# Doubles turned into floats with two VectorE operations a tile instead of four, and block sums and splits of the second MLP's input in smaller, spread pieces

## The chip, the core and the metric

The program runs on one core of a Trainium2 chip. Its time is that of one execution on the device in microseconds (us); lower is better. An execution was also recorded by the hardware profiler, and all rows below come from that one record.

The engines are TensorE (PE in the profile, with PEld for its weight loads), VectorE (DVE), ScalarE (ACT), GpSimd (POOL) and SyncE (SP), which here only issues DMAs. Each engine runs its own instructions in order; semaphores tie the engines together.

## The reference

```python
def _attn_ref(q, k, v, p):                       # (8, 8, 576, 64), p: (8, 8, 32, 64)
    def sm_attn(qq, kk, vv):
        s = scale * np.matmul(qq, kk.transpose(0, 1, 3, 2))
        s = s - np.max(s, axis=-1, keepdims=True)
        a = np.exp(s)
        a = a / (np.sum(a, axis=-1, keepdims=True) + 1e-09)
        return np.matmul(a, vv)
    p_packed = sm_attn(p, k, v)
    return sm_attn(q, p_packed, p_packed)

def _moe_ref(x, w_gate, w_val, w_out, rms_g):    # x: (4608, 512), d_ff 1536
    rms = np.sqrt(np.mean(x * x, axis=-1, keepdims=True) + 1e-06)
    xn = x / rms * rms_g
    g = xn @ w_gate
    silu = g * (1.0 / (1.0 + np.exp(-g)))
    return (silu * (xn @ w_val)) @ w_out

def _moe2_ref(x, w_in, w_out):                   # d_ff 2048
    h = x @ w_in
    g = h * (1.0 / (1.0 + np.exp(-1.702 * h)))
    return g @ w_out
```

Attention goes into MLP one, that into MLP two. The five weight matrices arrive as 64-bit floats, everything else as 32-bit floats; the output has 32-bit floats.

## The kernel before

The first part runs attention for four pairs of batches, and beside it MLP one: `prods` (L661) forms the products of the packed values with the gate and value weights (`ps_w`), `gateval` (L699) multiplies them by the attention weights (`ps_g`), and `project` (L737) applies `w_out` (`ps_o`) and adds into `acc`. Nearly every matmul operand is split into a high part (ScalarE's cast to `fp32r`) and a low part (a subtraction on VectorE or GpSimd), and three matmuls replace one.

The weights become floats in `words` (L119). A double is read as two 32-bit words, `top` and `low`. ScalarE writes |top| to the SBUF tile `w` (L127). VectorE takes the maximum with a least value into `m` (L128), shifts left by 5 and right by 2 (L129), puts the two uppermost bits of `top` back (L130), and joins three bits of `low` (L131), which writes `w`. `m`, named `between`, is a PSUM bank out of the pool `mm` of five banks, the same five that `ps_w`, `ps_g` and `ps_o` take. For the last pair of blocks of MLP two, which is converted while MLP two already runs, there is no such bank and `m` is `w` itself. `convert` (L134) calls `words` for 36 pieces of MLP one's weights, then ScalarE (L140) and GpSimd (L141) split `w`; `weights` (L851) calls it for 32 pieces of MLP two's. `raw` has three buffers, `w` two.

MLP two (`main`, L987) uses seven block products instead of eight for each of its two matrix products. It works on five spans of tokens, three of 2 x 512 and two of 2 x 384, and each span goes in four turns. A turn has 14 up steps (`up`, L1035: six matmuls into a bank `ps_up`) and seven down steps (`down`, L1101: 24 or 18 matmuls into banks `ps_dn`), interleaved by `form_at` and `down_at`; the down steps of a turn come during the turn after it. VectorE empties the banks (L1064 to L1073, L1149), and `form` (L1078) prepares the left operands (L1087 to L1091, L1095, L1096).

The input of a span is `b11`, `b12`, `b21`, `b22`, loaded by `load_x` (L1006), and the sums `t1 = b12 - b11`, `t3 = b22 - b12`, `t2 = b22 - t1`, `t4 = b21 - t2`. `prepare(s + 1, q)` (L1017) makes block `q` of the next span directly after the last up step that reads `q` of this one: in the last seven up steps of a span. It also computes the sums there, in place (L1024, L1028, L1029, L1031), and splits each whole block of 128 x 1024 or 128 x 768 with one ScalarE copy (L935) and one subtraction (L936), on GpSimd for `b11`, `b21`, `b22` and on VectorE for `t1` to `t4`.

In the last turn of a span, after down step 1, three additions on GpSimd add `acc["u"]` to three quarters of the result (L1150 to L1153). Steps 5 and 6 send the result out.

The order within each engine is made by a planner that simulates the program when it is built; it may move an instruction ahead of others that were written earlier, where its inputs and its buffers are there.

Of the kernel before, what the change touches and what calls it, by code (L numbers as in the profile page):

```python
# [9 lines left out]
F32 = mybir.dt.float32  # L10
F32R = mybir.dt.float32r
I32 = mybir.dt.int32
AF = mybir.ActivationFunctionType
ALU = mybir.AluOpType
# [2 lines left out]
DRAM = bass.MemoryType.DRAM  # L17


LEAST_WORD = 2.0**-15  # L20
GELU = 1.702


def fl(t):

    return t.bitcast(F32)
# [3 lines left out]
def tile_pack_attention__then__two_mlps(  # L30
# [14 lines left out]
    nc = tc.nc  # L45
# [9 lines left out]
    P = 128  # L55
# [29 lines left out]
    NGR = NP2 // 2  # L85
    TH = 512
    WHOLE = 3
    HALF = DM // 2
    spans = [(i * 2 * TH, TH) for i in range(WHOLE)]
# [29 lines left out]
    def words(pool, r, n, banks=None, bufs=2):  # L119

        top, low = r[:, :, 1], r[:, :, 0]
        w = pool.tile([P, n], I32, tag="w", name="w", bufs=bufs)
        wf = w.bitcast(F32)
        m = w if banks is None else banks.tile([P, 512], I32, tag="mm", name="between")[:, :n]
        nc.scalar.activation(wf, top.bitcast(F32), AF.Abs)  # L127
        nc.vector.tensor_scalar(m.bitcast(F32), wf, LEAST_WORD, None, op0=ALU.max)  # L128
        nc.vector.tensor_scalar(m, m, 5, 2, op0=ALU.logical_shift_left, op1=ALU.logical_shift_right)  # L129
        nc.vector.scalar_tensor_tensor(m, top, -(1 << 30), m, op0=ALU.bitwise_and, op1=ALU.bitwise_or)  # L130
        nc.vector.scalar_tensor_tensor(w, low, 29, m, op0=ALU.logical_shift_right, op1=ALU.bitwise_or)  # L131
        return w

# [697 lines left out]
    def mlp2(cv):  # L831
# [85 lines left out]
        def x_tile(q, n=TH):  # L917
            xb[q] = pools["pre"].tile([P, 2, 2, TH], F32R, tag=q, name=f"x_{q}", bufs=1)[:, :, :, :n]
            return xb[q]
# [13 lines left out]
        def split_x(q, src, engine, n=TH):  # L933
            t = x_tile(q, n)
            nc.scalar.copy(t[:, 0], src)  # L935
            engine.tensor_sub(t[:, 1], src, fl(t[:, 0]))  # L936
# [50 lines left out]
        def main(wp, sp, pm, pa, later):  # L987
            turns = [(s, g) for s in range(len(spans)) for g in range(NGR)]
            ups = [(t, a, q) for t in range(len(turns)) for a in range(2) for q in product_order]
            PER = 2 * len(product_order)  # L990
# [7 lines left out]
            def load_wo(d):  # L998
                if d < 7 * len(turns):
                    t, j = divmod(d, 7)  # L1000
                    wo[d] = wp.tile([P, 2, 2, HALF], F32R, tag="wo", name="wo2", bufs=WOB)
                    nc.sync.dma_start(fl(wo[d]), wo2_d[turns[t][1]][:, down_blocks.index(down_order[j][1])])

            xr = {}

            def load_x(s):  # L1006
                if s < len(spans):
                    t0, n = spans[s]
                    for q, i0, k in (("b11", 0, 0), ("b12", 0, 1), ("b22", 2, 1), ("b21", 2, 0)):
                        if q == "b21":  # L1010
                            t = wp.tile([P, 2, TH], F32, tag="xr", name="xr", bufs=1)
                        else:
                            t = cv.tile([P, 2, TH], F32, tag="raw", name="xr", bufs=RAWS)
                        xr[q] = t[:, :, :n]
                        load_part(xr[q], i0, t0 + k * n, n)

            def prepare(s, q):  # L1017

                if s == len(spans):
                    return  # L1020
                n = spans[s][1]
                b11, b12, b21, b22 = (xr[x] for x in ("b11", "b12", "b21", "b22"))
                if q == "t2":
                    nc.vector.tensor_sub(b11, b22, b11)  # L1024
                source = {"t1": "b11", "t2": "b11", "t3": "b12", "t4": "b21"}.get(q, q)
                split_x(q, xr[source], nc.gpsimd if q in ("b11", "b21", "b22") else nc.vector, n)
                if q == "b11":
                    nc.vector.tensor_sub(b11, b12, b11)  # L1028
                    nc.vector.tensor_sub(b12, b22, b12)  # L1029
                elif q == "b21":  # L1030
                    nc.vector.tensor_sub(b21, b21, b11)  # L1031

            g, bank, u2 = {}, {}, {}

# [64 lines left out]
            acc, banks = {}, {}  # L1099

            def down(d):  # L1101

                t, j = divmod(d, 7)
                s, gr = turns[t]
                t0, n = spans[s]
                per = n // P
                first, last = gr == 0, gr == NGR - 1
                which = "AB" if t % 2 == 0 else "BA"
                name, go_on = which[(0, 1, 0, 1, 0, 1, 0)[j]], j in (2, 5, 6)
                parts = [(r, min(2, per - r)) for r in range(0, per, 2)]  # L1110
                if not go_on:
                    banks[name] = [
                        pa.tile([P, 2, HALF], F32, tag=f"dn{name}{i}", name="ps_dn", bufs=1) for i in range(len(parts))
                    ]
                oh, ol = formed.pop(d)
                w = wo.pop(d)
                for o, (r0, m) in zip(banks[name], parts):
                    i = 0
                    for r in range(m):
                        for a in range(2):  # L1120
                            for x, y in ((oh, 0), (oh, 1), (ol, 0)):
                                nc.tensor.matmul(  # L1122
                                    o[:, r],
                                    x[:, a, (r0 + r) * P : (r0 + r + 1) * P],
                                    w[:, a, y],
                                    start=i == 0 and not go_on,
                                    stop=i == 6 * m - 1,
                                    skip_group_check=True,
                                )
                                i += 1  # L1130
                if first and j == 0:
                    for k in range(2):
                        acc[k] = sp.tile([P, TH // P, DM], F32, tag=f"acc{k}", name="acc2", bufs=1)
                    acc["u"] = sp.tile([P, TH // P, HALF], F32, tag="accu", name="accu", bufs=1)
                target, begins = {
                    0: ("u", True), 1: ("u", False), 2: ((0, 0), True), 3: ((1, 1), True),
                    4: ((1, 1), False), 5: ((0, 1), True), 6: ((1, 0), True),
                }[j]
                if target == "u":
                    to = acc["u"]  # L1140
                else:
                    k, c = target
                    to = acc[k][:, :, c * HALF : (c + 1) * HALF]
                for o, (r0, m) in zip(banks[name], parts):
                    z = to[:, r0 : r0 + m]
                    if first and begins:
                        nc.scalar.copy(z, o[:, :m])
                    else:
                        nc.vector.tensor_add(z, z, o[:, :m])  # L1149
                if last and j == 1:  # L1150
                    for k, c in ((1, 1), (0, 1), (1, 0)):
                        z = acc[k][:, :per, c * HALF : (c + 1) * HALF]
                        nc.gpsimd.tensor_add(z, z, acc["u"][:, :per])  # L1153
                if last and j >= 5:
                    k = j - 5
                    for r0, m in parts:
                        at0 = t0 + k * n + r0 * P
                        nc.sync.dma_start(
                            out[at0 : at0 + m * P, :].rearrange("(r p) d -> p r d", p=P), acc[k][:, r0 : r0 + m]
                        )  # L1160
# [2 lines left out]
                load_wi(c)  # L1163
            for d in range(WOB):
                load_wo(d)
            form_at, down_at = {}, {}
            for d in range(7 * len(turns)):
                t, j = divmod(d, 7)
# [3 lines left out]
            for c in range(len(ups) + PER + LAG):  # L1172
                if c < len(ups):
                    up(c)
                    load_wi(c + WIB)
                    if c >= 7:
                        next(later, None)
                    if c % PER == 6 and turns[ups[c][0]][1] == NGR - 2:
                        load_x(turns[ups[c][0]][0] + 1)
                for d in form_at.get(c, ()):  # L1180
                    form(d)
                for d in down_at.get(c, ()):
                    down(d)
                    load_wo(d + WOB)
# [4 lines left out]
    with ExitStack():  # L1189
# [8 lines left out]
        cv = ctx.enter_context(tc.tile_pool(name="cv", bufs=1, side="left"))  # L1198
        with ExitStack() as st1:
# [56 lines left out]
            u, ahead, calm, since = 0, None, 0.0, 0.0  # L1256
# [95 lines left out]
```

## Time and profile before

| | |
|---|---|
| time, median of 3 runs | 1658.5 us (1656.1 to 1660.7) |
| the profiled execution | 1658.6 us |
| its span, first to last instruction | 1656.7 us |
| busy share of the span | PE 97%, PEld 92%, DVE 70%, ACT 52%, POOL 56% |
| mean granted TensorE clock | 0.992 of full speed |
| moved by DMA | 348.21 MB, 210 GB/s on the mean |

Busy shares are means over stages of different kind. A wait names the instruction that was late and the one that released it. The granted clock is given as a share of full speed; 0.5 stands for the lower of the two levels, 1.2 GHz, and 1.0 for the upper, 2.4 GHz.

### The profile page before, as it was taken

The numbers are of one execution on the slowest core, as the hardware profiler recorded it, in microseconds if no ns is written. First come the engines' busy times: TensorE is split into PE (matmuls) and PEld (weight loads), VectorE is DVE, ScalarE is ACT, GpSimd is POOL, SyncE is SP. The second block draws the span as 40 slices with busy tenths as digits, with TensorE's granted clock in tenths as the row PEclk, the third lists the DMA queues.
The fourth block names the chain that finished last, engine by engine and source line by source line (L and its number), as shares of the span: only waits on it lengthen the run. The fifth ranks groups of instructions, "written<-read, shape, count | busy, mean of one in ns | idle before, by whom it ended". The sixth has DMA issues, their size and how long they took to land.

```text
span 1656.7 us, 29176 instructions
## 1 busy us (share of the span) xinstructions
PE 1611.8 (97%) x10608; PEld 1516.4 (92%) x10608; DVE 1161.9 (70%) x2004; ACT 866.7 (52%) x1771; POOL 928.8 (56%) x744
## 2 busy tenths in 40 slices
PE   7899999999999999999999999999999999999997
PEld 5689998999999999999999889899989999999997
DVE  5788988877768777686886476864585458567564
ACT  4667776666566666665655344434344434434432
POOL 2447777656666557562665266564456446546444
PEclk8999999999999999999999999999999999999999
DMA  9655666584565855465445878676667667887874
GB/s 256 178 163 173 205 189 221 190 254 150 167 204 204 271 186 186 148 207 205 167 177 175 293 259 268 218 245 187 188 207 242 192 186 243 281 250 237 286 222 127
DMA packets 217726, 348.21 MB, mean 210 GB/s; under 512 B 93936, under 2 KB 123632, under 8 KB 211440
## 3 DMA queue, kind: packets, MB, share of 16 engines
q1 hardware_dynamic: 217584, 346.35, 65.1%
q8 instruction: 85, 1.39, 0.3%
q14 instruction: 57, 0.47, 0.1%
HBM read 279.19 MB, written 67.11 MB: 209 GB/s over the span
## 4 chain that ended last, share of the span: by engine, by line
PE 77%; DVE 11%; issue 3%; POOL 3%; DMA 3%; ACT 3%; SPq 0%; POOLq 0%; DVEq 0%; ACTq 0%
PE ps_dn L1122 18%; PE ps_up L1051 18%; PE ps_o L748 15%; PE ps_g L712 13%; PE ps_w L679 3%; PE ps_at L308 3%; PE ps_at L353 2%; PE ps_at L297 2%; PE ps_at L443 2%; DMA vn<-in_v_dram 1%; DVE x_t L936 1%; DVE Wl L684 1%; DVE w L131 1%; POOL Hl L734 0%; DVE between L128 0%
## 5 line engine op out<-in xcount | busy, mean ns | idle before, releaser
L1096 POOL TENSOR_TENSOR ol<-g,oh 128x1024 fp32r<-128x1024 f32 (+1 forms) x120 | 267.2, 2237 | 310.4 <-ACT oh L1095 305.2
L1122 PE MATMUL ps_dn<-wo,oh 128*128 128x256 f32 x2016 | 368.3, 284 | 2.3 <-ACT oh L1095 1.3
L1122 PEld LDWEIGHTS ps_dn<-wo,oh 128*128 128x128 f32 x2016 | 319.9, 192 | 10.2 <-ACT oh L1095 2.0
L748 PE MATMUL ps_o<-Hh,wo 128*128 128x384 f32 x1152 | 321.5, 340 | 2.8 <-ACT Hh L733 1.2
L1122 PE MATMUL ps_dn<-wo,ol 128*128 128x256 f32 x1008 | 278.9, 285 | 3.3 <-POOL ol L1096 3.3
L712 PE MATMUL ps_g<-Aqh,Wh 128*128 128x288 f32 x768 | 232.6, 303 | 6.0 <-DVE th L722 1.5
L712 PE MATMUL ps_g<-Aql,Wh 128*128 128x288 f32 x768 | 226.1, 295 | 0.0
L712 PE MATMUL ps_g<-Aqh,Wl 128*128 128x288 f32 x768 | 225.6, 295 | 0.0
L1051 PE MATMUL ps_up<-x_t,wi 128*128 128x512 f32 (+1 forms) x936 | 215.0, 369 | 7.3 <-DVE g L1073 6.0
L748 PEld LDWEIGHTS ps_o<-Hh,wo 128*128 128x128 f32 x1152 | 210.0, 188 | 8.0 <-ACT Hh L733 2.0
L734 POOL TENSOR_TENSOR Hl<-th,Hh 128x576 fp32r<-128x576 f32 x96 | 139.3, 1452 | 134.4 <-ACT Hh L733 134.1
L748 PE MATMUL ps_o<-Hl,wo 128*128 128x384 f32 x576 | 194.6, 338 | 1.4 <-POOL Hl L734 1.3
L1122 PEld LDWEIGHTS ps_dn<-wo,ol 128*128 128x128 f32 x1008 | 190.7, 193 | 4.4 <-POOL ol L1096 3.7
L1051 PEld LDWEIGHTS ps_up<-x_t,wi 128*128 128x128 f32 x936 | 165.8, 188 | 27.2 <-DVE g L1073 7.1
L684 DVE TENSOR_TENSOR Wl<-ps_w,Wh 64x512 fp32r<-64x512 f32 x192 | 131.7, 686 | 73.1 <-ACT Wh L683 70.6
L1074 ACT ACTIVATE g<-g 128x512 f32<-128x512 f32 (+1 forms) x120 | 70.3, 589 | 206.8 <-DVE g L1071 114.2
L763 POOL TENSOR_TENSOR acc<-acc,add 128x384 f32<-128x384 f32 x135 | 139.0, 1041 | 53.9 <-ACT add L761 52.8
L1095 ACT CAST oh<-g 128x1024 fp32r<-128x1024 f32 (+1 forms) x120 | 113.5, 961 | 103.4 <-PE ps_dn L1122 70.8
L1051 PE MATMUL ps_up<-x_b,wi 128*128 128x512 f32 (+1 forms) x702 | 164.4, 368 | 0.0
L712 PEld LDWEIGHTS ps_g<-Aqh,Wh 128*128 128x128 f32 x768 | 144.0, 188 | 12.0 <-DVE th L722 1.8
L1149 DVE TENSOR_TENSOR acc<-acc,ps_dn 128x512 f32<-128x512 f32 (+1 forms) x160 | 99.2, 630 | 77.9 <-PE ps_dn L1122 73.2
L683 ACT CAST Wh<-ps_w 64x512 fp32r<-64x512 f32 x192 | 111.4, 580 | 78.7 <-PE ps_w L679 46.4
(203 smaller groups left out, 3363.0 us busy)
## 6 DMA issues: line engine op xcount, KB each, us to landing
wo<-wo SPq DMA_DIRECT2D x188, 512.0 KB, 3.9
wi<-wi SPq DMA_DIRECT2D x274, 256.0 KB, 3.7
wg<-wg SPq DMA_DIRECT2D x48, 1024.0 KB, 6.2
raw<-in_moe_w_out_dram SPq DMA_DIRECT2D x28, 512.0 KB, 4.3
wi<-stage SPq DMA_DIRECT2D x24, 512.0 KB, 3.6
wo<-stage SPq DMA_DIRECT2D x24, 512.0 KB, 3.6
x<-acc SPq DMA_DIRECT2D x32, 288.0 KB, 3.4
vn<-in_v_dram SPq DMA_DIRECT2D x16, 512.0 KB, 7.2
```

What stands on the lines that cost most here:

```text
L683: nc.scalar.copy(Wh[rows, :, g], src)
L684: nc.vector.tensor_sub(Wl[rows, :, g], src, fl(Wh[rows, :, g]))
L712: nc.tensor.matmul(ps, st[:, o, g, c * P : (c + 1) * P], mv[:, g, cols], start=n == 0, stop=n == 3 * NG - 1)
L734: nc.gpsimd.tensor_sub(Hl, th, fl(Hh))
L748: nc.tensor.matmul(ps, st[:, m * P : (m + 1) * P], mv[:, cols], start=n == 0, stop=n == 3 * len(ss) - 1)
L763: nc.gpsimd.tensor_add(a, a, t)
L1051: nc.tensor.matmul(o, w[:, y, k], x[:, z, k], start=i == 0 and not go_on, stop=i == 5, skip_group_check=bool(go_on))
L1074: nc.scalar.activation(gf, o if q == "a12" else gf, AF.Gelu_apprx_sigmoid)
L1095: nc.scalar.copy(oh, src)
L1096: nc.gpsimd.tensor_sub(ol, src, fl(oh))
L1122: nc.tensor.matmul(o[:, r], x[:, a, (r0 + r) * P : (r0 + r + 1) * P], w[:, a, y], start=i == 0 and not go_on, stop=i == 6 * m - 1, skip_gr ...
L1149: nc.vector.tensor_add(z, z, o[:, :m])
```

## The change

In `words`, ScalarE's function becomes Prelu with scale 2^-112 and slope -2^32 for negative values, and it writes into `m` instead of `w`. That gives the exponent its new bias, and a negative word becomes a positive one with 32 more in the exponent, which the shift left by 3 turns into the sign. VectorE does that shift and the join with `low`. In MLP two the sums leave `prepare` for `sums`, called at up steps 10 and 13 of the third turn and 2 of the fourth; `t1` has a tile of its own, `t2` two half tiles. `prepare` splits by halves and in four instructions. The additions of `acc["u"]` come one each after down steps 2, 3 and 4, in the last span on VectorE.

```diff
-        nc.scalar.activation(wf, top.bitcast(F32), AF.Abs)
-        nc.vector.tensor_scalar(m.bitcast(F32), wf, LEAST_WORD, None, op0=ALU.max)
-        nc.vector.tensor_scalar(m, m, 5, 2, op0=ALU.logical_shift_left, op1=ALU.logical_shift_right)
-        nc.vector.scalar_tensor_tensor(m, top, -(1 << 30), m, op0=ALU.bitwise_and, op1=ALU.bitwise_or)
+        nc.scalar.activation(m.bitcast(F32), top.bitcast(F32), AF.Prelu, scale=REBIAS, alpha=NEGATIVE)
+        nc.vector.tensor_scalar(m, m, 3, None, op0=ALU.logical_shift_left)
         nc.vector.scalar_tensor_tensor(w, low, 29, m, op0=ALU.logical_shift_right, op1=ALU.bitwise_or)
...
+            def sums(s, q):
...
+                if q == "t1":
+                    xr[q] = wp.tile([P, 2, TH], F32, tag="xt", name="xr", bufs=1)[:, :, :n]
+                    nc.vector.tensor_sub(xr[q], xr["b12"], xr["b11"])
+                elif q == "t3":
+                    nc.vector.tensor_sub(xr["b12"], xr["b22"], xr["b12"])
+                else:
+                    xr[q] = [cv.tile([P, TH], F32, tag="w", name="xr", bufs=2)[:, :n] for _ in range(2)]
+                    for k in range(2):
+                        nc.vector.tensor_sub(xr[q][k], xr["b22"][:, k], xr["t1"][:, k])
...
+                src = xr[{"t3": "b12", "t4": "b21"}.get(q, q)]
+                t = x_tile(q, n)
+                for k in range(2):
+                    part = src[k] if q == "t2" else src[:, k]
+                    nc.scalar.copy(t[:, 0, k], part)
+                    (nc.gpsimd if q[0] == "b" else nc.vector).tensor_sub(t[:, 1, k], part, fl(t[:, 0, k]))
+                if q == "b21":
+                    for k in range(2):
+                        nc.vector.tensor_sub(src[:, k], src[:, k], xr["t2"][k])
...
-                if last and j == 1:
-                    for k, c in ((1, 1), (0, 1), (1, 0)):
-                        z = acc[k][:, :per, c * HALF : (c + 1) * HALF]
-                        nc.gpsimd.tensor_add(z, z, acc["u"][:, :per])
+                if last and 2 <= j <= 4:
+                    k, c = ((0, 1), (1, 1), (1, 0))[j - 2]
+                    z = acc[k][:, :per, c * HALF : (c + 1) * HALF]
+                    (nc.vector if s + 1 == len(spans) else nc.gpsimd).tensor_add(z, z, acc["u"][:, :per])
...
+            EARLY = {10: "t1", 13: "t3", 16: "t2"}
...
+                    s, at = turns[ups[c][0]][0], (turns[ups[c][0]][1] - NGR + 2) * PER + c % PER
+                    if at == 6:
+                        load_x(s + 1)
+                    elif at in EARLY:
+                        sums(s + 1, EARLY[at])
```

## Rows read from the trace of the kernel before

**Rows 1.** Page: busy us, share of the span and instructions of each engine.
```profile
PE 1611.8 (97%) x10608; PEld 1516.4 (92%) x10608; DVE 1161.9 (70%) x2004; ACT 866.7 (52%) x1771; POOL 928.8 (56%) x744
```
**Rows 2.** Windows: stretch, length, busy us (instructions) by engine, clock, DMA share, GB/s.
```profile
0.00:83.00 83.00, 67.67 (x293) 48.50 (x294) 55.20 (x126) 44.83 (x128) 27.25 (x50) 0.91 0.79 216
83.00:300.00 217.00, 211.09 (x1422) 198.47 (x1421) 188.49 (x401) 154.12 (x365) 149.53 (x150) 0.99 0.61 191
300.00:924.00 624.00, 617.48 (x4194) 598.73 (x4192) 465.03 (x915) 371.93 (x848) 367.79 (x365) 1.00 0.58 192
924.00:1657.00 733.00, 715.52 (x4704) 670.66 (x4702) 453.17 (x564) 295.79 (x432) 384.18 (x179) 0.99 0.72 230
```
**Rows 3.** Waits of PE, whole span: us in total, times, longest.
```profile
PE ps_up L1051 <- DVE g L1073: 6.0, 3, 2.4
PE ps_at L297 <- DVE kn L200: 5.6, 1, 5.6
...
PE ps_dn L1122 <- POOL ol L1096: 3.3, 2, 2.8
...
PE ps_w L679 <- DVE w L131: 0.5, 1, 0.5
```
**Rows 4.** Groups by line: count | busy us, mean ns | idle before, releasers.
```profile
L127 ACT ACTIVATE w<-raw 128x512 f32<-128x512 f32 x68 | 46.0, 676 | 35.3 <-DMA raw<-in_moe_w_in_dram 11.9 <-DMA raw<-in_moe_w_out_dram 11.8 <-POOL wo L141 7.4
...
L452 ACT ACTIVATE ps_at<-ps_at 128x256 f32<-128x256 f32 (+1 forms) x80 | 29.6, 370 | 15.5 <-PE ps_at L443 14.4
...
L128 DVE TENSOR_SCALAR between<-w 128x512 f32<-128x512 f32 x64 | 44.0, 687 | 2.3 <-ACT w L127 1.5 <-ACT ps_at L452 0.2
...
L130 DVE SCALAR_TENSOR_TENSOR w<-raw,w 128x512 int32<-128x512 int32 x4 | 4.8, 1198 | 0.1
```
**Rows 5.** Windows, only instructions on `between`: stretch, length, DVE busy, clock, DMA.
```profile
0.00:83.00 83.00, 20.52 (x31) 0.91 0.79 216
83.00:300.00 217.00, 77.85 (x115) 0.99 0.61 191
300.00:924.00 624.00, 76.03 (x111) 1.00 0.58 192
```
**Rows 6.** Chain of waits, 83 to 300 us: shares by line.
```profile
by line: PE ps_o L748 21.3%; PE ps_g L712 12.3%; DMA vn<-in_v_dram 6.6%; issue 4.7%; PE ps_w L679 4.6%; PE ps_at L443 3.9%; PE ps_at L353 3.7%; PE ps_at L297 3.1%; DVE th L727 2.9%; DVE th L725 2.8%; POOL Hl L734 2.5%; DVE between L128 2.0%
```
**Rows 7.** Timeline of DVE, 1016 to 1066 us: start, us, line, [idle before].
```profile
1016.52 0.69 DVE L1149 TENSOR_TENSOR acc<-acc,ps_dn 128x512 f32<-128x512 f32 x1 [2.10 <-PE ps_dn L1122]
...
1046.78 1.23 DVE L1028 TENSOR_TENSOR xr<-xr 128x1024 f32<-128x1024 f32 x1
1048.04 3.31 DVE L1029 TENSOR_TENSOR xr<-xr 128x1024 f32<-128x1024 f32 x1
...
1054.80 1.21 DVE L1024 TENSOR_TENSOR xr<-xr 128x1024 f32<-128x1024 f32 x1
...
1065.97 1.27 DVE L1073 TENSOR_TENSOR g<-u,ps_up 128x512 f32<-128x512 f32 x2
```
**Rows 8.** Timelines of POOL and DVE, 1628 to 1648 us.
```profile
1628.95 0.95 DVE L1089 TENSOR_TENSOR g<-s,g 128x768 f32<-128x768 f32 x1
...
1634.89 2.25 DVE L1091 TENSOR_TENSOR g<-g 128x768 f32<-128x768 f32 x1
...
1638.81 5.42 POOL L1153 TENSOR_TENSOR acc<-acc,accu 128x768 f32<-128x768 f32 x3
1644.20 3.57 POOL L1096 TENSOR_TENSOR ol<-g,oh 128x768 fp32r<-128x768 f32 x2
```
**Rows 9.** Window at the end, columns as in Rows 2.
```profile
1646.00:1652.40 6.40, 6.30 (x28) 6.04 (x28) 1.82 (x4) 0.00 (x0) 1.77 (x1) 0.52 0.33 123
```
**Rows 10.** Chain of waits, 1490 to 1540 us: start, us, what.
```profile
1520.20 3.35 PE ps_dn L1122 x28
```
**Rows 11.** Groups by line, ACT: table loads.
```profile
L162 ACT ACT_TABLE_LOAD x1 | 1.3, 1283 | 0.7 <-PEq L1336 0.7
L720 ACT ACT_TABLE_LOAD x1 | 1.3, 1283 | 0.0
```

More of the change, by code (lines that the diff above doesn't have):

```diff
@@ L17 @@
 DRAM = bass.MemoryType.DRAM
-LEAST_WORD = 2.0**-15
+REBIAS = 2.0**-112
+NEGATIVE = -(2.0**32)
 GELU = 1.702
@@ L124, in words @@
         w = pool.tile([P, n], I32, tag="w", name="w", bufs=bufs)
-        wf = w.bitcast(F32)
         m = w if banks is None else banks.tile([P, 512], I32, tag="mm", name="between")[:, :n]
-        nc.scalar.activation(wf, top.bitcast(F32), AF.Abs)
-        nc.vector.tensor_scalar(m.bitcast(F32), wf, LEAST_WORD, None, op0=ALU.max)
-        nc.vector.tensor_scalar(m, m, 5, 2, op0=ALU.logical_shift_left, op1=ALU.logical_shift_right)
-        nc.vector.scalar_tensor_tensor(m, top, -(1 << 30), m, op0=ALU.bitwise_and, op1=ALU.bitwise_or)
+        nc.scalar.activation(m.bitcast(F32), top.bitcast(F32), AF.Prelu, scale=REBIAS, alpha=NEGATIVE)
+        nc.vector.tensor_scalar(m, m, 3, None, op0=ALU.logical_shift_left)
         nc.vector.scalar_tensor_tensor(w, low, 29, m, op0=ALU.logical_shift_right, op1=ALU.bitwise_or)
@@ L1015, in load_x @@
                         load_part(xr[q], i0, t0 + k * n, n)
+            def sums(s, q):
+                if s == len(spans):
+                    return
+                n = spans[s][1]
+                if q == "t1":
[7 more added lines that the diff above has]
+                        nc.vector.tensor_sub(xr[q][k], xr["b22"][:, k], xr["t1"][:, k])
             def prepare(s, q):
@@ L1021, in prepare @@
                 n = spans[s][1]
[L1022 to L1031, printed above, removed]
+                src = xr[{"t3": "b12", "t4": "b21"}.get(q, q)]
[7 more added lines that the diff above has]
+                        nc.vector.tensor_sub(src[:, k], src[:, k], xr["t2"][k])
             g, bank, u2 = {}, {}, {}
@@ L1177, in main @@
                         next(later, None)
-                    if c % PER == 6 and turns[ups[c][0]][1] == NGR - 2:
-                        load_x(turns[ups[c][0]][0] + 1)
+                    s, at = turns[ups[c][0]][0], (turns[ups[c][0]][1] - NGR + 2) * PER + c % PER
[3 more added lines that the diff above has]
+                        sums(s + 1, EARLY[at])
                 for d in form_at.get(c, ()):
```

## The prediction

> **What bounds the kernel now.** The page comes first: PE is busy 97% of the span, VectorE 70%, the others less [rows 1]. So the floor is TensorE, and no edit here removes a matmul. What can be won is PE's idle time, and the clock it loses by idling. The windows say where that is [rows 2]: PE idles 83.0 - 67.67 = 15.3 us up to 83 us, 5.9 up to 300, 6.5 up to 924 and 17.5 in MLP two; of the first, 5.6 us is the wait for the first load [rows 3], which stays. VectorE is next to the bound only between 83 and 300 us, at 188.49 of 217 us. The waits of PE then tell what ends the gaps. In MLP two the largest is an up bank that VectorE empties late (L1073), 6.0 us in three places, and then a low part that GpSimd makes late at the end (L1096), 3.3 us with 2.8 in one place [rows 3]. In the conversions PE hardly waits directly: 0.5 us for a bank that the join (L131) frees.
>
> **The conversions.** Each of 68 calls loses two of four VectorE instructions. In a bank one takes 77.85 / 115 = 0.68 us [rows 5] (L128: 0.687 [rows 4]), so some 68 x 2 x 0.68 = 92 us of VectorE's 1161.9 go. The four calls without a bank lose a slower L130 (1.2 us each [rows 4]); I count nothing more for them.
>
> How much of it does PE get? Below: on `between` VectorE spends 20.52 of 55.20, 77.85 of 188.49 and 76.03 of 465.03 us in the three stages [rows 2, 5]; half of that is 19%, 21% and 8% of its work. If PE's idle time shrank by those shares it would be 9.7 x 0.19 + 5.9 x 0.21 + 6.5 x 0.08 = 3.5 us. Above: all of the idle time, 9.7 + 5.9 + 6.5 = 22.1 us. The chain lies between: of the removed instructions L128 alone holds 2.0% of 217 = 4.3 us of it in the second stage [rows 6], but behind it PE itself or ScalarE is next late. I take 5 us. It could also be a loss, for the reason given under the first rival.
>
> Prelu is not in this trace. On ScalarE a 128 x 512 tile from SBUF to SBUF takes 0.676 us, and half as wide a tile from bank to bank 0.37 [rows 4]; so Prelu into a bank costs between 0.37 and 2 x 0.37 = 0.74 us, and I take 0.68, no difference. ScalarE is busy 154.12 of 217 us in the fullest stage and covers it. Prelu now takes the bank, and the wait for a free `w` (POOL 7.4 us [rows 4]) moves from ScalarE's L127 to VectorE's L131: behind it in VectorE's queue stand the evictions of `ps_g` and `ps_w`, for which PE waits. I count that inside the 5 us.
>
> **The boundaries between spans.** Around 1047 to 1066 us VectorE does three sums among its evictions, 1.23 + 3.31 + 1.21 = 5.75 us, and a late pair of L1073 without any idle time before it [rows 7]. All three leave this stretch. Splitting by halves gives a little back: 128 x 512 takes 0.69 us, 128 x 1024 1.21 [rows 7], so 0.17 us for each of five instructions, 0.85 us. VectorE arrives 4.9 us earlier where PE lost at most 2.4: the 6.0 us go whole, and what is late next is nothing but PE. Bounds: 0 if another engine's half is late instead, 6.0. The extra ScalarE copies and GpSimd halves (seven and three more a boundary) lie beside PE, on engines with 295.79 and 384.18 of 733 us busy [rows 2].
>
> The sums come back in the third and fourth turns. Each of the two whole ones takes 1.2 to 3.3 us, the dear one being the one that coincides with GpSimd's work [rows 7]. VectorE there has pauses like 2.10 us before an eviction [rows 7]; a sum of 3.31 is 1.2 us longer. If each such excess stalled PE, four boundaries with two sums would cost 9.7 us; but at the boundary VectorE ran 5.75 us of sums and cost PE 2.4 at most, so a single one should hide behind banks not yet needed. I take 0.5 us (bounds 0 and 9.7).
>
> **The end.** After down step 1 of the last turn GpSimd does the three additions, 5.42 us, and only then the last two low parts [rows 8]; PE waits 2.8 us for the first of them [rows 3]. Then comes the dearer half: after that idle stretch the last 28 matmuls run at a granted clock of 0.52, the lower level of 1.2 GHz, and take 6.30 us [rows 9], where 28 of the same take 3.35 at other places [rows 10]. Without the additions GpSimd is free 5.4 us earlier, the wait is gone, and with it the reason for the low clock: 2.8 + 2.95 = 5.75 us. VectorE gets three additions of 128 x 768, each 0.95 us alone and 2.25 beside GpSimd [rows 8], 2.9 to 6.8 us. Queued behind them are its readings of the down banks of steps 3 and 4, and steps 5 and 6 accumulate in those banks. Replacing 9.0 us of GpSimd's row by so much, with VectorE busy 1.82 of the last 6.40 us [rows 9], I charge 0.25 us (bounds 0 and 2 x 1.3 = 2.6, if two of them are slow and nothing covers them). In the other spans the additions stay on GpSimd, spread, and no wait of PE stands on them: nothing. The bounds of the whole end are 0 and 5.75 of gain; whether the clock holds is the larger part.
>
> **The sum.** 5.0 + 6.0 + 5.75 - 0.5 - 0.25 = 16.0 us off. The profiled execution took 1658.6 us (1656.7 of span and 1.9 around it), 0.1 above the median of the runs shown, so it is set against the median as it is: 1642.6 us. MLP two alone gives 11.0 of it.
>
> **Rivals.**
>
> *Prelu holds a bank while it waits.* Now L127 writes SBUF and waits for its raw doubles 11.9 + 11.8 = 23.7 us [rows 4] without any bank. Afterwards the same wait stands in front of an instruction that has one of the five banks, and the next matmul on this bank comes later. If all of it reached PE and VectorE's relief brought nothing: 1658.6 - 11.0 + 23.7 = 1671.3, slower. It decides from 16 of the 23.7 us on. For it: PE already waits for `between`, 0.5 us. Against: that is all it waits, and the bank's own use falls from four VectorE instructions to two. 0.06.
>
> *Prelu is not with Exp and Tanh.* There are two table loads in the whole trace, of 1.283 us [rows 11], so Abs, Exp, Tanh, Square and copies share one table. If Prelu did not, each call would switch there and back: 8, 29 and 28 calls in the three stages (a quarter of the counts in [rows 5]). In the second that puts 29 x 2.57 = 74 us on ScalarE's 154.12, 11.6 more than the 217 us; in the first 20.5 us, half of them taken as on the path, 10.3. 1658.6 - 11.0 + 11.6 + 10.3 = 1669.5. 0.03. The Trainium skill, "ScalarE: Activation LUTs", section "Table sets: the hidden batching unit", says that cheap functions are in every set as filler and names relu, copy, identity and abs, not Prelu; the trace agrees for abs and copy, and no run so far shows Prelu.
>
> *VectorE is off the path in the conversions.* Then only MLP two pays: 1658.6 - 11.0 = 1647.6. For it: PE's direct wait of 0.5 us; against: the chain's 2.0%. 0.22.
>
> *The boundary only changes its wait.* The planner may put the free sums where they hurt, or a ScalarE half is late: the 6.0 us stay. 1658.6 - 5.0 - 5.5 + 0.5 = 1648.6. 0.12.
>
> *Only the end pays,* 1658.6 - 5.5 + 0.5 = 1653.6: 0.06.
>
> *The start opens up.* Earlier joins let GpSimd and the loads run ahead, and 14 of the 22.1 us go: 1633.6. 0.07.
>
> **How the numbers follow.** The forecast has 0.44 and its own range is 1638 to 1647. Measurement tells 0.3%, 5.0 us. Faster are the forecast, the two cases near 1648 and the open start, 0.85, of which 0.03 ends above 1653.5 after all: 0.82. Same: 0.06 + 0.03 = 0.09. Slower: 0.06 + 0.03 = 0.09. The range goes from 1634, where half of the open start is left out, to 1654, past the case of the end alone; what lies beyond is about 0.15, and the unknown 9.7 and 2.6 us of VectorE's moved work are inside it.
>
> **What would show it.** Right: two VectorE rows of 64 conversions at 0.68 us and VectorE's busy time near 1070 us; ScalarE's conversions at 0.6 to 0.75 us and still two table loads; no L1073 among PE's longest waits in MLP two; a last window at clock 1.0 with its 28 matmuls in 3.4 us; PE's idle time before 924 us down by 3 to 8 us. Wrong: new waits of PE behind the early sums in the third turns, waits of `ps_g`, `ps_w` or `ps_o` for the join, a PE wait for step 4's reading by VectorE near the end, or the same idle time before 924 us although VectorE has 90 us less to do.

## The result, and the profile after

The change takes the kernel from 1658.5 us (1656.1 to 1660.7, five runs) to **1642.5 us** (1639.5 to 1643.1, five runs): ratio 0.9897, interval 0.9883 to 0.9912. Forecast was 1642.6. The number came out and its terms did not: the conversions are worth over four times what they were given, and the boundaries between spans of MLP two, which were to give 5.5 us, cost 10.

The profiled execution of after took 1639.52 us, the shortest of the five; so the traces differ by 19 us where the medians differ by 16. Its page, first line, answers to [rows 1]:

```profile
PE 1599.6 (98%) x10608; PEld 1514.1 (92%) x10608; DVE 1098.9 (67%) x1895; ACT 872.0 (53%) x1799; POOL 927.6 (57%) x753
```

VectorE is 63 us less busy, where 92 were forecast. The durations did fall so: in the kernel with only the new `words` (below) those of all VectorE instructions sum to 1163.7 us, before to 1254.7. But instructions that follow each other overlap a little (below, one of 2.30 us starts at 1033.30 and the next at 1035.53), and the page counts that time once: there 1091.3 us. In after the sums take longer (41.0 us by groups of lines, before 31.0), and the last span's three additions are VectorE's, 5.4 us; that more than makes up the rest. PE's own busy time is 12 us less for the same 10,608 matmuls. So part of the gain was never in PE's idle time; it was inside what is counted as busy.

The windows of after, columns as in [rows 2] (MLP two now begins near 900 us):

```profile
0.00:83.00 83.00, 71.40 (x353) 52.85 (x353) 53.17 (x125) 51.72 (x149) 33.79 (x58) 0.98 0.84 242
83.00:300.00 217.00, 216.99 (x1487) 209.18 (x1487) 166.17 (x359) 161.77 (x377) 157.91 (x156) 1.00 0.63 196
300.00:915.00 615.00, 610.38 (x4139) 593.36 (x4137) 428.25 (x837) 361.70 (x821) 351.17 (x352) 1.00 0.60 199
915.00:1638.00 723.00, 700.78 (x4635) 658.67 (x4633) 451.26 (x575) 296.83 (x454) 384.73 (x188) 0.99 0.71 225
```

Look at the counts of matmuls: by 300 us 353 + 1487 = 1840 are done, before 293 + 1422 = 1715 [rows 2]. Between 83 and 300 us PE's idle time fell by 5.9 us, to nothing, and the mean of a matmul fell from 211.09 / 1422 = 148.4 to 145.9 ns, another 3.7 us over 1487. A part of that is the clock, 0.99 before and 1.00 in after. From 86 to 300 us it is 1.00 in both, with 208.09 us for 1415 matmuls before and 214.00 for 1470 in after: 147.1 against 145.6 ns, 2.2 us over 1470. So waits too short to appear as gaps stand inside "busy". In MLP two PE now idles 22.2 of 723 us, before 17.5 of 733.

PE's waits in after, whole span: us in total, times, longest, as in [rows 3]:

```profile
PE ps_dn L1136 <- DVE accu L1163: 5.8, 2, 5.0
PE ps_at L297 <- DVE kn L200: 5.4, 1, 5.4
PE ps_up L1065 <- DVE g L1080: 5.3, 1, 5.3
PE ps_g L712 <- DVE th L722: 2.7, 2, 1.6
PE ps_dn L1136 <- ACT oh L1109: 2.5, 2, 1.6
...
PE ps_dn L1136 <- DVE acc L1163: 1.4, 1, 1.4
PE ps_up L1065 <- DVE g L1087: 1.1, 2, 0.7
```

The old boundary wait (L1073 before, L1087 now) has shrunk from 6.0 to 1.1 us, and the wait for GpSimd's last low part is no longer there; both were forecast. In their place stand two single waits of 5.3 and 5.0 us for VectorE. Where the first comes from is seen in VectorE's timeline of after at the boundary between spans 0 and 1 (start, us, line, [idle before]); [rows 7] show the same place before:

```profile
1033.30 2.30 DVE L1045 TENSOR_TENSOR xr<-xr 128x512 f32<-128x512 f32 x1
1035.53 2.31 DVE L1024 TENSOR_TENSOR xr<-xr 128x1024 f32<-128x1024 f32 x1
...
1047.36 2.32 DVE L1026 TENSOR_TENSOR xr<-xr 128x1024 f32<-128x1024 f32 x1 [1.13 <-DMA xr<-x]
1049.61 5.61 DVE L1030 TENSOR_TENSOR xr<-xr 128x512 f32<-128x512 f32 x2
1055.14 0.68 DVE L1078 TENSOR_TENSOR u<-u,ps_up 128x512 f32<-128x512 f32 x1
1055.85 0.69 DVE L1080 TENSOR_TENSOR g<-u,ps_up 128x512 f32<-128x512 f32 x1
```

L1024, L1026 and L1030 are `t1`, `t3` and `t2`. These here do not belong to span 1, whose sums ran at 976 to 982 us; they are those of span 2, whose blocks ScalarE first copies at 1183 us. The program writes them in the third and fourth turns of span 1, and the planner moved them, with their loads, to where the tiles became free: into the very boundary that the change was to clear. VectorE does 10.2 us of sums there instead of 5.75, and L1026 and L1030 keep it for 7.9 us before it turns to the banks that PE waits for (L1078, L1080). PE then idles and its clock falls with it (windows of after, columns as in [rows 2]):

```profile
1051.30:1056.60 5.30, 0.01 (x2) 0.01 (x1) 5.21 (x4) 0.00 (x0) 3.37 (x2) 0.72 0.35 100
1056.60:1062.00 5.40, 5.40 (x25) 4.82 (x26) 4.30 (x6) 2.20 (x3) 2.26 (x1) 0.64 0.17 49
```

First 5.3 us without matmuls, then 5.4 us at a granted clock of 0.64. The 5.0 us stand at the next boundary, near 1216 us, with the sums of span 3 ahead of L1163.

The conversions, groups by line: count | busy, mean ns | idle before. They answer to [rows 4] and [rows 11]:

```profile
L129 ACT ACTIVATE between<-raw 128x512 f32<-128x512 f32 x64 | 41.3, 645 | 6.4 <-DVE th L725 2.4 <-DVE th L727 1.7 <-DVE Wl L684 1.2
L130 DVE TENSOR_SCALAR between<-between 128x512 int32<-128x512 int32 x64 | 44.3, 692 | 11.5 <-ACT between L129 10.5
L131 DVE SCALAR_TENSOR_TENSOR w<-raw,between 128x512 int32<-128x512 int32 x64 | 43.4, 678 | 1.0
L162 ACT ACT_TABLE_LOAD x1 | 1.3, 1283 | 0.7 <-PEq L1354 0.7
L720 ACT ACT_TABLE_LOAD x1 | 1.3, 1283 | 0.0
```

Prelu into a bank takes 0.645 us. Its wait for raw doubles, 23.7 us before, is gone, so no bank is held during one. There are two table loads as before: Prelu needs none of its own.

### The profile page after: what moved, and what is told of

The parts are those of the page before. It is cut to its first block, busy times and chain, and to the rows that moved or that the text cites. A ratio compares the mean times of both kernels' runs of the same rounds, so it can differ in the third digit from the quotient of the medians.

```text
span 1637.7 us, 29088 instructions
## 1 busy us (share of the span) xinstructions
PE 1599.6 (98%) x10608; PEld 1514.1 (92%) x10608; DVE 1098.9 (67%) x1895; ACT 872.0 (53%) x1799; POOL 927.6 (57%) x753
## 4 chain that ended last, share of the span: by engine, by line
PE 90%; DVE 5%; issue 1%; DMA 1%; ACT 1%; POOL 0%; SPq 0%; POOLq 0%; DVEq 0%; ACTq 0%
PE ps_dn L1136 20%; PE ps_up L1065 19%; PE ps_o L748 19%; PE ps_g L712 18%; PE ps_w L679 4%; PE ps_at L308 3%; PE ps_at L297 3%; PE ps_at L353 2%; PE ps_at L443 2%; DVE xr L1030 1%; PE ps_at L341 1%; DVE x_t L1042 1%; DMA xr<-x 1%; DVE xr L1045 0%; PE ps_at L281 0%
## 5 line engine op out<-in xcount | busy, mean ns | idle before, releaser
L1110 POOL TENSOR_TENSOR ol<-g,oh 128x1024 fp32r<-128x1024 f32 (+1 forms) x120 | 269.4, 2255 | 301.0 <-ACT oh L1109 300.1
L1163 DVE TENSOR_TENSOR acc<-acc,ps_dn 128x512 f32<-128x512 f32 (+1 forms) x160 | 99.6, 630 | 72.3 <-PE ps_dn L1136 68.0
```

The lines of the kernel that those rows point to most:

```text
L1110: nc.gpsimd.tensor_sub(ol, src, fl(oh))
```

## The experiments

All ratios are against the kernel before, run on the same chip; before's median in these was between 1657.9 and 1658.8 us. The leads are in us: the start of the n-th of the 10,608 matmuls, subtracted from its start in the trace of before. The 5,800th stands just ahead of MLP two, the 9,800th behind its last boundary.

| | n = 300 | 1800 | 5800 | 7000 | 8200 | 9800 | last |
|---|---|---|---|---|---|---|---|
| after | 11.4 | 20.3 | 25.0 | 20.1 | 14.5 | 15.7 | 19.4 |
| only `words` | 10.8 | 19.7 | 24.3 | 24.3 | 24.2 | 24.3 | 24.3 |
| all but `words` | 0.1 | -1.0 | -1.5 | -11.9 | -20.2 | -19.0 | -15.2 |
| sums pinned | 10.8 | 19.8 | 24.4 | 27.9 | 30.7 | 33.8 | 37.6 |

**Only the conversions.** Before, with the new `words` and nothing else:

```diff
-        nc.scalar.activation(wf, top.bitcast(F32), AF.Abs)
-        nc.vector.tensor_scalar(m.bitcast(F32), wf, LEAST_WORD, None, op0=ALU.max)
-        nc.vector.tensor_scalar(m, m, 5, 2, ...)
-        nc.vector.scalar_tensor_tensor(m, top, -(1 << 30), m, ...)
+        nc.scalar.activation(m.bitcast(F32), top.bitcast(F32), AF.Prelu, scale=REBIAS, alpha=NEGATIVE)
+        nc.vector.tensor_scalar(m, m, 3, None, op0=ALU.logical_shift_left)
```

> The kernel before with only the conversion in words changed (Prelu and two VectorE instructions). Between the two traces the first up step of MLP two moved from 923.7 to 898.4 us, 25.3 earlier, where the prediction had 5. Theory: the conversions alone make that, and MLP two keeps the 733.0 us it had, so 1658.5 - 25.3 = 1633, below the changed kernel's 1642.5. Rival: part of the 25 us is the start of one execution (8 us are there by the 150th matmul) and does not come back in the median: 1638 to 1643.

1635.5 us, ratio 0.9862 (0.9842 to 0.9882): 22.4 us off, more than the whole change gives, and between the theory and its rival. (The first up step of after stands at 898.7 us in the trace, so it comes 25.0 us earlier, not 25.3.)

**All but the conversions.** After, with the old `words`.

> The changed kernel with the old conversion in words: only the sums, the splits by halves and the additions at the end are changed. Theory (the planner draws the sums of the span after next into the boundary): MLP two takes 739 instead of 733 us, the end pays some 4 of it back already, so 1658.5 + 6 = 1665, slower than before. Rival (the longer MLP two goes with the earlier start and other positions of the converted weights, not with the sums): 1647 to 1654, the prediction's 11 us less or a part of them.

1672.0 us, ratio 1.0075 (1.0052 to 1.0098): 14.1 us slower than before, where 6 were expected. In PE's waits of this kernel (lines stand one lower than in after):

```profile
PE ps_dn L1137 <- DVE accu L1164: 8.2, 2, 7.4
...
PE ps_up L1066 <- DVE g L1081: 5.3, 1, 5.3
PE ps_up L1066 <- DVE g L1086: 3.9, 2, 2.6
```

The same two boundaries, and dearer than in after, whose larger waits are 5.0 and 5.3. So the halves do not add: -22.4 + 14.1 = -8.3, measured together -16.0. The planner plans the whole program anew for each kernel.

**The sums pinned.** After, with the three kinds of sums held at their written place:

```diff
-                    nc.vector.tensor_sub(xr[q], xr["b12"], xr["b11"])
+                    tc.keep_in_program_order(nc.vector.tensor_sub(xr[q], xr["b12"], xr["b11"]))
...
```

> The changed kernel with its four sums (t1, t3, two halves of t2) held behind everything written earlier for VectorE, so that they come at up steps 10, 13 and 16 and not a boundary earlier. Theory (position): the two PE waits of 5.3 and 5.0 us at the first two boundaries and the 1.6 at the third go, 1642.5 - 12 = 1630.5 (1628 to 1633). Rival (the sums cost the same anywhere, since two-input instructions collide with GpSimd in the third turn as well, or the halves themselves make the boundary longer): 1640 to 1644.

1621.5 us, ratio 0.9774 (0.9758 to 0.9791): 21 us better than after with the same instructions, and below both expectations. The theory added up waits (12 us) and left out the low clock behind them: the mean granted clock is 0.994 to 0.995 in the runs of after and 0.998 to 0.999 in these, which over 1640 us is another 6 us or so (an estimate from these figures). VectorE's timeline of this kernel has the sums of span 2 where the program says, 111 us later than in after:

```profile
1146.48 1.22 DVE L1024 TENSOR_TENSOR xr<-xr 128x1024 f32<-128x1024 f32 x1
...
1153.46 1.22 DVE L1026 TENSOR_TENSOR xr<-xr 128x1024 f32<-128x1024 f32 x1
...
1164.13 4.61 DVE L1030 TENSOR_TENSOR xr<-xr 128x512 f32<-128x512 f32 x2
```

and the boundary's window holds no idle time and no low clock, in this kernel

```profile
1012.00:1060.00 48.00, 48.00 (x310) 43.80 (x309) 38.06 (x46) 24.57 (x37) 30.62 (x15) 1.00 0.75 233
```

against, in after,

```profile
1012.00:1060.00 48.00, 41.48 (x253) 36.93 (x252) 39.68 (x43) 20.73 (x31) 26.79 (x14) 0.93 0.62 204
```

310 matmuls instead of 253. That a sum costs the same wherever it stands falls; its place decides.

**Only the additions at the end.** Before, with the additions of `acc["u"]` as in after.

> The kernel before with only the additions of acc u moved: one each after down steps 2, 3 and 4, in the last span on VectorE. Theory: the 2.84 us wait for the low part goes, the last 28 matmuls run at the upper clock (2.95 us), and 1.4 us of a new wait stay as in the changed kernel: 1658.5 - 4.4 = 1654.1. Rival (the prediction's sum): 1658.5 - 5.5 = 1653.0. Second rival (the clock does not hold, or the rows of one execution are chance): 1657 to 1659.

1655.7 us, ratio 0.9981 (0.9969 to 0.9992): 2.1 us off, half of what was expected. At the end of its trace the last 42 matmuls run at full clock:

```profile
1645.40:1651.00 5.60, 5.34 (x42) 5.07 (x42) 4.88 (x9) 0.00 (x0) 1.24 (x1) 1.00 0.16 60
```

The end gives its 4 us (the lead goes from -2.5 at the 9,800th matmul to 1.5 at the last), but the new plan has lost 3.2 us ahead of it, among them a new wait of 1.5 us for ScalarE in `ps_g`, nowhere near the edit. So a new plan alone can move the time by 2 to 3 us (4.4 expected less 2.1 by the medians, 3.2 in this trace), and differences of that size between the kernels below cannot be put down to their edits.

**One or two VectorE instructions given back, outside the chain.** In the kernel with only `words`, after the join:

```diff
+        for i in range(1):      # range(2) in the second kernel
+            nc.vector.tensor_reduce(spare_max[:, i : i + 1], w.bitcast(F32), axis=AX.X, op=ALU.max)
```

> The kernel before with the new words, and after each join one more VectorE instruction that only reads w (a maximum over 128 x 512 into one number a partition, some 0.67 us; its result is not used). It gives back half of the VectorE time saved, but delays neither the float tile nor the bank. Theory A (VectorE's time made the 22.4 us): half is lost, about 1647. Theory B (the shorter chain from the double to the float tile made them): 1635 to 1637. Theory C (the planner's new order is chance): anything between 1630 and 1660, not in line with the run with two.

> The same with two such instructions after each join, so that VectorE has as many instructions a tile as before. Theory A (VectorE's time): nearly all is lost, 1654 to 1660. Theory B (the shorter chain): 1635 to 1640. Theory C (chance of the order): not in line with the run with one.

1647.0 us with one (0.9928, 0.9911 to 0.9944) and 1649.0 with two (0.9940, 0.9919 to 0.9960). One (0.67 us each, 46 us of VectorE) gives back 11.5 of the 22.4 us (10.6 if each kernel is set against before on its own chip). The second gives back 2 more, which is not clear of noise: the runs lie between 1646.2 and 1650.0 us with one and between 1646.9 and 1653.6 with two. The first result fits theory A; the second fits neither A nor B. VectorE's time matters, and not in proportion.

**A longer chain without VectorE.** In the kernel with only `words`, between Prelu and the shift:

```diff
+        for _ in range(2):
+            nc.scalar.copy(m.bitcast(F32), m.bitcast(F32))
```

> The kernel before with the new words, and two ScalarE copies of the bank onto itself between Prelu and the shift (some 0.55 us each), so that the chain from the double to the float tile and the hold of the bank are about as long as before, while VectorE keeps its two instructions. ScalarE gets some 75 us more. Theory A (VectorE's time): 1635 to 1640, as long as ScalarE does not become the bound between 83 and 300 us, where it would be busy about 190 of 217 us. Theory B (the shorter chain): the gain is gone, 1652 to 1658.

1642.6 us (0.9896, 0.9879 to 0.9912): 0.59 us each, 80 us on ScalarE, give back 7.1 us (6.2 against before on its own chip), between the two theories. The bank is held 1.2 us longer, and ScalarE loses slack too; the run does not part these.

**Both given back.** Two shifts by nothing on the bank, on VectorE, between shift and join; this is before's number of VectorE instructions in before's place:

```diff
+        for _ in range(2):
+            nc.vector.tensor_scalar(m, m, 0, None, op0=ALU.logical_shift_left)
```

> The kernel before with the new words, and two more VectorE instructions on the bank itself between the shift and the join (shifts by 0, 0.69 us each): VectorE's time and the chain's length are as before, only Prelu in place of the absolute value and the bank taken one ScalarE instruction earlier are new. In e5_two_more the same VectorE time outside of the chain gave back 13.5 of 22.4 us, in e6_longer_chain the chain without VectorE's time 7.1. Theory (time and chain together are the whole): 1655 to 1660. Rival (the join and what follows did not depend on the chain, the rest comes from what Prelu does without, the wait for a free w on ScalarE): 1647 to 1651.

1654.4 us (0.9974, 0.9963 to 0.9985): only 4.3 us are left, close to the theory. The window from 83 to 300 us tells the same in the rows. First this kernel, then the one with two outside the chain, then only `words`:

```profile
83.00:300.00 217.00, 212.26 (x1423) 198.14 (x1422) 191.04 (x406) 153.97 (x362) 149.11 (x147) 1.00 0.61 189
```

```profile
83.00:300.00 217.00, 212.16 (x1443) 201.35 (x1442) 194.51 (x412) 155.61 (x364) 149.71 (x148) 1.00 0.60 184
```

```profile
83.00:300.00 217.00, 216.99 (x1488) 209.17 (x1486) 166.71 (x360) 161.92 (x378) 157.32 (x155) 1.00 0.63 195
```

With the two in the chain PE does 1423 matmuls in this window, as before did 1422; without them 1488. The first two rows have the same busy time of PE and differ by 20 matmuls: idle time alone would not have told them apart. What is left stands ahead of this window; the first 83 us of the kernel with two in the chain, columns as in [rows 2], have 328 matmuls instead of before's 293, at a clock of 0.98 instead of 0.91:

```profile
0.00:83.00 83.00, 68.78 (x328) 49.63 (x328) 57.51 (x133) 49.19 (x143) 30.28 (x56) 0.98 0.80 223
```

**Only MLP one's pieces.** The new `words` in `convert`, 36 of 68 calls; the old one for MLP two's weights.

> The kernel before with the new words only for the 36 pieces of MLP one's weights (up to 300 us); MLP two's 32 pieces keep four VectorE instructions. In the traces 20 of the 24 us by which the conversions lead at 910 us are there at 315 us. Theory (the gain belongs to the stretch where VectorE is 87% busy): 1657.9 - 19 = 1639, some 3 us above the run with all 68. Rival (all calls count alike): half, 1646.

1640.6 us (0.9887, 0.9868 to 0.9905): 18 of the 22.4 us come from these 36 pieces. That agrees with the leads, 20 us by the 1800th matmul.

**The additions pinned as well, and whole blocks.** The pinned kernel with the last span's three additions also held in program order; and the pinned kernel with `prepare` splitting whole blocks again, only `t2` by halves.

```diff
-                    (nc.vector if s + 1 == len(spans) else nc.gpsimd).tensor_add(z, z, acc["u"][:, :per])
+                    i = (nc.vector if s + 1 == len(spans) else nc.gpsimd).tensor_add(z, z, acc["u"][:, :per])
+                    if s + 1 == len(spans):
+                        tc.keep_in_program_order(i)
```

> The changed kernel with the sums held in their place as in e3_pinned, and in the last span the three additions of acc u held behind the evictions written before them. Theory (the planner put two additions, 4.2 us, ahead of an eviction that step 4 waits for): the 1.4 us wait at the end goes, 1621.5 - 1.4 = 1620. Rival (the wait only moves to step 6, which needs the eviction of step 4): 1621 to 1622.

> The same as e3_pinned, but prepare splits b11, b12, b21, b22 and t1, t3, t4 as whole blocks again (only t2, which has two tiles, stays in halves). Theory (the place of the sums is what counts): the same as e3_pinned, 1621 to 1623. Rival (the short pieces matter, since a whole one stands 2.8 us before an eviction when GpSimd collides): 1624 to 1628, with PE waits for L1073's successor at the first two boundaries.

1620.3 us (0.9768, 0.9747 to 0.9790) and 1623.8 us (0.9789, 0.9768 to 0.9811). The first is the best version; the 1.4 us wait for L1163 at the end is gone from its trace. The second is 2.3 us slower than with halves (1.6 against before on its own chip), between theory and rival. PE waits in three places for the eviction that the rival named (L1090 is L1087 of after), 1.6 us that the kernel with halves does not have:

```profile
PE ps_up L1068 <- DVE g L1090: 1.6, 3, 0.6
```

## Why the prediction was right by its number and wrong by its steps

In the traces, before to after: MLP two's first up step comes at 898.7 us instead of 923.7, so the stages ahead of it give **25.0 us**; MLP two lasts 1637.7 - 898.7 = 739.0 us instead of 1656.7 - 923.7 = 733.0. Forecast were 5.0 for the first and 11.0 for the second.

**The conversions: mis-sized.** The step that failed is "PE's idle time shrank by those shares", and the ceiling beside it, "all of the idle time, 9.7 + 5.9 + 6.5 = 22.1 us". The trace passed that ceiling. PE's idle time counts only gaps; what VectorE delays by a fraction of a matmul stands inside the busy time, and the clock lost after a gap does too. By the rows up to 300 us, before against after, idle time gives (83.00 - 67.67) - (83.00 - 71.40) + 5.9 = 9.6 of the 20.3 us of lead at the 1800th matmul. The clock gives some 0.07 x 83 + 0.01 x 217 = 8 (an estimate from the two clocks of each row), and the shorter matmuls at full clock the rest. The sum had no term for the second and the third. The mechanism holds: VectorE's two instructions, where they stand in the chain of a bank, account for 18.1 to 18.9 of 22.4 us (1654.4 against 1635.5; by the differences to before 4.3 remain). VectorE's time alone brings 10.6 to 13.5 of it, a longer chain alone 6.2 to 7.1. "VectorE off the path in the conversions" falls.

The remaining 4 us lie early: with both instructions back the lead is 6.4 us at the 150th matmul and between 3 and 8 from there to the end, 5.3 at the last. The clock at the start is enough to make them. From 15 to 20 and from 20 to 25 us, before and then after:

```profile
15.00:20.00 5.00, 3.35 (x15) 2.48 (x16) 2.88 (x6) 3.42 (x12) 0.00 (x0) 0.72 1.09 347
20.00:25.00 5.00, 5.00 (x13) 3.21 (x12) 3.92 (x8) 1.46 (x4) 1.68 (x2) 0.50 1.01 221
```

```profile
15.00:20.00 5.00, 4.89 (x19) 3.91 (x20) 3.14 (x6) 3.44 (x10) 0.83 (x1) 0.66 1.09 354
20.00:25.00 5.00, 5.00 (x26) 3.30 (x24) 2.30 (x8) 2.14 (x6) 2.33 (x3) 1.00 1.17 243
```

In both the clock falls before 20 us; in the kernel before it then stays at the lower level, in after it is back at the upper one. From 20 to 25 us PE is busy all 5 us in both and does 13 matmuls in one, 26 in the other. All three traces with the old `words` have 0.50 there, all ten with Prelu 0.85 to 1.00, the one with both instructions back 0.97. Over its first 83 us that one has 0.98 against 0.91, which is worth up to 0.07 x 83 = 5.8 us (an estimate) and so covers the 4. Its ten runs, at a mean clock of 0.995 to 0.998 against 0.989 to 0.995 in the runs of before beside them, point the same way.

The number of VectorE's instructions is not the reason, since that kernel has as many as before. What differs in the traces is ScalarE's order. Before, its second |top| comes ahead of the copy `aTh`, for which PE waits 0.94 us at 17.6 us; with Prelu, in all ten traces, the second conversion comes behind it (before, then after):

```profile
17.59 0.68 ACT L127 ACTIVATE w<-raw 128x512 f32<-128x512 f32 x1
18.15 0.37 ACT L162 COPY aTh<-ps_at 128x256 f32<-128x256 f32 x1
```

```profile
17.06 0.37 ACT L162 COPY aTh<-ps_at 128x256 f32<-128x256 f32 x1
...
17.91 0.65 ACT L129 ACTIVATE between<-raw 128x512 f32<-128x512 f32 x1
```

That this order makes the clock come back is not shown by a run of its own, nor why the planner orders Prelu so. The rival "the start opens up" had this place, at 0.07.

**The boundaries: wrong in sign.** "All three leave this stretch" failed. They left it for the next span and came back for the one after, brought forward by the planner. "VectorE arrives 4.9 us earlier" is true only of the pinned kernel, where the boundaries gain 33.8 - 24.4 = 9.4 us (5.5 were forecast) and PE waits for none of the sums in the third and fourth turns. In after, MLP two without its end is some 10 us longer: 6.0 us as it is, and 3.9 more that the end has given. The waits of 5.3 and 5.0 us and the low clock behind them more than replace the 6.0 us. The rival "the planner may put the free sums where they hurt" named this, at 0.12, and then priced it as no gain; that the same VectorE time can hurt more at a boundary than before, with sums pulled in from a later turn, was not worked out. The bound of 9.7 us that was kept for sums in the third turns would have been the size.

**The end: right, less a second wait.** The wait for L1110 and the low clock are gone: the last 42 matmuls take 5.4 us at clock 1.00.

```profile
1626.00:1627.40 1.40, 0.00 (x0) 0.00 (x0) 1.40 (x3) 0.00 (x0) 1.40 (x2) 1.00 0.00 0
1627.40:1633.00 5.60, 5.40 (x42) 5.14 (x42) 4.89 (x9) 0.00 (x0) 1.32 (x1) 1.00 0.15 54
```

But the 0.25 us charged for VectorE's additions are 1.4: in its timeline two of them, beside GpSimd, stand ahead of the reading that step 4 waits for.

```profile
1622.85 4.17 DVE L1167 TENSOR_TENSOR acc<-acc,accu 128x768 f32<-128x768 f32 x2
1626.94 1.34 DVE L1163 TENSOR_TENSOR acc<-acc,ps_dn 128x256 f32<-128x256 f32 x3
```

2.8 + 2.95 - 1.4 = 4.3 us, of which 0.4 is lost again between the last matmul and the end. The forecast was 5.5.

**Together:** forecast -5.0, -5.5, -5.5; in the traces -25.0, +9.9, -3.9, which is -19.0, and -16.0 between the medians. Two errors of 20 and 15 us cancelled, and that the number came out is luck. The prediction is no evidence that its sum was understood.

**Prelu's two rivals** fall: two table loads, and no wait of PE for a bank held by it.

## What to carry to other kernels

An engine that delays the bound one by a little each time does not show in the idle time: compare the number of matmuls done by a given time, and the mean of one, with another stretch of the same work. Work that becomes free to move early will be moved early by a planner that starts what is ready; say which earlier stretch has the inputs and the buffers for it, and hold it in its place if that stretch is full (21 us here, for three wrapped calls). A change in two parts is to be run as its parts: here one was worth -22.4 and the other +14.1.

## What was not expected of the hardware

Of the clock: after the 5.3 us without a matmul it was 0.64 over the next 5.4 us; after the 1.4 us near the end it stayed at 1.00. Near the start, where PE is idle in small pieces, nearly the same work was followed by different clocks: before, 3.35 us of work between 15 and 20 us, at 0.72, by 5 us at 0.50; in the kernel with the sums pinned, 3.60 us, at 0.73, by 5 us at 0.93.

VectorE's subtraction of two SBUF tiles of 128 x 512 took 5.61 us for two at 1049 us, where GpSimd worked, and 1.28 us for two at 980 us, after GpSimd's instruction there had ended. The Trainium skill, "SBUF — State Buffer", section "SBUF: two separate sides", says that a VectorE operation with two SBUF inputs and a GpSimd operation that reads SBUF take a shared pair of ports in turn, each for its whole length; the sizes here agree with that, though no run varied it. So a sum's place can matter twice: by what is queued behind it and by what GpSimd does beside it.
